# An attention and network kernel on one core: its first output products by half chunk, its raw weights in shorter rows, and its first four steps in a new order

## The chip, the cores and the metric

The kernel runs on one core of a Trainium2 chip. The core has five engines that run beside each other: TensorE (matrix products), VectorE, ScalarE, GpSimd and SyncE (which here only issues transfers), and 16 DMA engines that move data between HBM and the on-chip memory. Results of TensorE stand in banks called PSUM, everything else in SBUF. The metric is the device time of one execution in microseconds. Before the change it is 602.12 us, the median of 3 runs (602.03 to 602.43).

## The reference

A gated recurrence, whose result is the input of a two-layer network:

```
f = 1/(1+exp(-f_logit))                     # B=4, H=8, S=768, D=48
for t in range(S):
    state = f[:,:,t,:,None]*state + k[:,:,t]^T v[:,:,t]     # (B,H,D,D)
    y[:,:,t] = q[:,:,t] @ state
x = y.transpose(0,2,1,3).reshape(3072, 384)
h = x @ w_in                                # w_in 384 x 2048
g = max(h,0) + alpha*min(h,0)
out = g @ w_out                             # w_out 2048 x 384
```

q, k, v, f_logit are f32; w_in and w_out are stored as f64, eight bytes a value.

## The kernel before

The recurrence is computed in chunks of 128 positions. Two batches make a pair, so there are 2 pairs × 6 chunks = 12 steps of 256 tokens each, numbered 0 to 11. Within a chunk the state is not formed for each position: products of q with k (both scaled with running products of f) give a matrix A of weights that is nonzero where the key is not later than the query, and one product of A with the values gives the output of the chunk. The matrix falls into blocks of 32 and half chunks of 64 positions: nearby keys (`scores`), keys of an earlier block of the same half, and, through the state, everything before. All products are f32.

The work of a step is written as Python generators, each `yield` ending an item:

- P, `prepare`: the loads of f, q, k and v, then the sigmoid on ScalarE (L314), products and scans on VectorE (L326 to L468), the A copies of scaled queries on ScalarE (L473).
- S and T, `scores` for the first and second batch of the pair: an item of 32 products of q and k (L592), an item of VectorE's masked copies into `ad` (L601), another 32 products (L592 again, other operands), another masked copy (L627 in chunk 0, L611 later).
- O, `carry`: products across halves (in chunk 0 those of L509, copied to `ad` by L514), across 32-blocks (L524, copied to A by L531), in chunk 0 the keys transposed on TensorE (L541) and copied by ScalarE (L545, `ksn`), the states (L555), and `moved`, which adds the state to the values `vs` (L565, L569 on VectorE; L571, a ScalarE copy, for the first half of chunk 0).
- Y, `attend`: four copies of `ad` into A on ScalarE (L635), the 32 output products (L646: A against values and state), the copies y (L653), and the transposition to xT: in step 0 by products with a 0/1 matrix on TensorE (L665) with copies L667, in the others by transfers (L676).
- K and M: the keys of later chunks, transposed by transfers (L483) and put in place (L491).
- n, `network`: eight items, each with a bank `ph` of products xT × w_in (L691), the negative part on ScalarE (`neg`, L696) and the gate on VectorE (L698). Then the second layer: in step 0 32 plain products (L711), a part in each of four items; in the later steps, a scheme with seven products of half matrices instead of eight (L730), whose sums of the gates are formed on VectorE (L777).

The weights arrive in 16 pieces, eight of w_in and eight of w_out, each 128 partitions × 768 values of eight bytes. An item `a` (w_in) or `b` (w_out), generator `upper`, issues the load of a piece on SyncE (L248) and has ScalarE make two numbers of it (L252, `lead`, and L253); an item `w` or `g` adds these on VectorE (L262) into the f32 weights. The pool has RAWS = 3 raw buffers and LEADS = 4 for `lead`; a fourth load waits until ScalarE has read the first. The first 16-bit word of a row carries only low bits and is left out, so the row begins at the second word: 2,046 bytes for w_in (three rows a partition) and 6,142 for w_out (one). W forms the sums of w_out for the seven-product scheme, X gives the banks of the early stage to the network. Two sorts of products have no use but to keep TensorE at work: i (L802, 128×256) and j (L810, 16 short ones).

The order of all this is written out by hand. `START` lists the items of the first steps, word by word (`P0:2` is two items of P of step 0), and `USUAL` repeats from step 5 on. TensorE, VectorE, ScalarE and SyncE execute their instructions in just this order (`tc.manual_schedule`), each waiting where an operand isn't ready; GpSimd follows program order. An item that stands early for one engine stands early for all four.

Of the kernel before, what the change touches and what calls it, by code (L numbers as in the profile page):

```python
# [17 lines left out]
C = 128  # L18
# [3 lines left out]
U = 2  # L22
CH = 64
NC2 = C // CH
NB = DB // 4
WP = 768
RAWS, LEADS = 3, 4
UP = 2.0 ** 16

BEGUN = 5  # L30
START = (
# [7 lines left out]
)  # L39
USUAL = "T:2 S:2 n:3 M n T:2 S n P+ S n P+ n:3 Y O P+ O:2 Y O n P+ Y:2 P+ n:3 P+:3 K+"  # L40

# [19 lines left out]
def kernel(  # L61
# [30 lines left out]
    nc = tc.nc  # L92
    B, NC, _, HP, _ = qT.shape
    DM = v.shape[-1]
    H = 2 * HP
    D = DM // H
# [4 lines left out]
    W = U * HP * C  # L101
# [22 lines left out]
    pairs = [psa.tile([128, 2, 512], F32, tag=f"pair{n}", name=f"pair{n}") for n in range(2)]  # L124
    more = [psb.tile([128, 2, 512], F32, tag=f"more{n}", name=f"more{n}") for n in range(2)]
# [8 lines left out]
    def bank(name):  # L134
        return net["pool"].tile([128, 512], F32, tag="net", name=name)
# [11 lines left out]
    vs = []  # L147
# [36 lines left out]
    for half in range(2):  # L184
        for m in range(1, NQ):
            n = NQ - m
# [7 lines left out]
    A = const.tile([128, U, H, C], F32, tag="A", name="A")  # L194
# [10 lines left out]

    first["raw"] = stage.tile([128, WP, 4], I16, tag="raw", name="w_in_raw0", bufs=RAWS)

# [9 lines left out]
    def load_weights(dst, src, name):  # L217

        rows_ = NK if dst is w_in_sb else 1
        pieces_ = dst.shape[1] * dst.shape[2] // WP  # L230
        if rows_ == 1:
            dst = dst.rearrange("p a n -> p (a n)").unsqueeze(1)
        width = WP // rows_
        words = src.rearrange("p (a n) -> p a n", a=rows_).bitcast(I16)
        got = {}

        def of(n):
            return dst[:, :, n * width:(n + 1) * width]

        def by_row(t):  # L240
            return t.rearrange("p (a n) -> p a n", a=rows_)

        def upper(n):
            if not n and dst is w_in_sb:
                raw = first["raw"]
            else:
                raw = stage.tile([128, WP, 4], I16, tag="raw", name=f"{name}_raw{n}", bufs=RAWS)
            nc.sync.dma_start(out=raw.rearrange("p (a n) four -> p a (n four)", a=rows_)[:, :, 0:4 * width - 1],  # L248
                              in_=words[:, :, 4 * n * width + 1:4 * (n + 1) * width])

            lead = stage.tile([128, WP], F16, tag="lead", name=f"{name}_lead{n}", bufs=LEADS)
            nc.scalar.activation(lead, raw[:, :, 2].bitcast(BF16), AF.Copy, scale=0.5)  # L252
            nc.scalar.activation(as_int(n, I32), by_row(raw.bitcast(U32)[:, :, 0]), AF.Copy, scale=2.0 ** -13)  # L253
            got[n] = lead

        def as_int(n, dtype):
            t = of(n).bitcast(dtype)
            return t if dtype is I32 else t.rearrange("p a (n two) -> p a n two", two=2)[:, :, :, 1]

        def both(n):  # L260
            t = by_row(got.pop(n).bitcast(I16))
            nc.vector.tensor_tensor(as_int(n, I16), as_int(n, I16), t, ALU.add)  # L262

        def uppers():
            for n in range(pieces_):
                upper(n)
                yield

        def rests():
            for n in range(pieces_):  # L270
                both(n)
                yield

        return uppers(), rests()
# [355 lines left out]
    def attend(bp, c, x):  # L630

        i = f"{bp}_{c}"
        for j in range(NJ):
            s_ = slice(DB * j, DB * (j + 1))
            nc.scalar.copy(A[s_].rearrange("p u h t -> p (u h) t")[:, :, s_], ad[s_].rearrange("p u r h t -> p (u r h) t"))  # L635
            if j % 2:
                yield

        py = (more if (bp, c) == steps[0] else pairs)[0]
        for u in range(U):  # L640
            for hp in range(HP):
                for cc in range(NC2):
                    for par in range(2):
                        hd = 2 * hp + par
                        o = hp * C + CH * cc
                        nc.tensor.matmul(py[64 * par:64 * par + 64, u, o:o + CH],  # L646
                                         lhsT=vs[bp][:, cc, u, hd * D:hd * D + 64],
                                         rhs=A[:, u, par * HP + hp, CH * cc:CH * (cc + 1)],
                                         start=True, stop=True)
        yield  # L650
        y = work.tile([128, U, HP, C], F32, tag="ksn", name=f"y_{i}", bufs=1)
        for u in range(U):
            nc.scalar.copy(y[:, u].rearrange("p h t -> p (h t)"), py[:, u])  # L653
        if c < NC - 1:
            x["moved"](1)
        xT = x["T"] = work.tile([128, NK, T], F32, tag="xT", name=f"xT_{i}")
        if not (bp or c):

            yield
            for kt in range(NK):  # L660
                b = bank(f"xt{kt}_{i}")
                these = [hp for hp in range(HP) if 2 * D * hp < 128 * (kt + 1) and 2 * D * (hp + 1) > 128 * kt]
                for hp in these:
                    o = 2 * D - 2 * D * hp + 128 * kt
                    nc.tensor.matmul(b[:, 0:T], lhsT=dense[:, o:o + 128], rhs=y[:, :, hp],  # L665
                                     start=(hp == these[0]), stop=(hp == these[-1]))
                nc.scalar.copy(xT[:, kt], b[:, 0:T])  # L667
            yield
            return
        queues = iter([nc.sync, nc.scalar, nc.gpsimd, nc.sync, nc.scalar] * 2)  # L670
        for hd in range(H):
            d = hd * D
            while d < (hd + 1) * D:
                n = min((hd + 1) * D, (d // 128 + 1) * 128) - d
                p0 = 64 * (hd % 2) + d - hd * D
                next(queues).dma_start(  # L676
                    out=xT[d % 128:d % 128 + n, d // 128].rearrange("p (u t) -> p u t", u=U),
                    in_=y[p0:p0 + n, :, hd // 2])
                d += n
        yield  # L680
# [132 lines left out]
    steps = [(bp, c) for c in range(NC) for bp in range(B // U)]  # L813
# [8 lines left out]
    with tc.manual_schedule(engines={mybir.EngineType.PE, mybir.EngineType.DVE, mybir.EngineType.Activation,  # L822
                                     mybir.EngineType.SP}):
        run = {}
        for n, step in enumerate(steps):
            x = {}
            for key, stage_ in zip("POYKMn", (prepare, carry, attend, keys_moved, landed, network)):
                run[key, n] = stage_(*step, x)
            run["S", n], run["T", n] = (scores(u, *step, x) for u in range(U))
        for key in ORDER:  # L830
            next(run[key] if key in run else pieces[key[0]])
# [55 lines left out]
```

## Time and profile before

| | |
|---|---|
| timed runs, median (lowest to highest) | 602.12 us (602.03 to 602.43) |
| profiled execution | 606.02 us |
| its span on the core | 604.2 us |
| granted TensorE clock, mean | 0.994 |
| TensorE busy | 579.1 us (96%) |
| VectorE busy | 495.1 us (82%) |
| ScalarE busy | 246.7 us (41%) |
| GpSimd busy | 83.6 us (14%) |
| DMA | 50.36 MB in 52,880 packets, mean 83 GB/s |

The profile is of one execution. Its lines name the engine, the line of the kernel, the operation, output and inputs by the program's names, the tile's size and the number of instructions; a timeline's rows begin with start and busy time in microseconds and end with the idle time ahead of the row and what ended it. One f32 product shows as two records on TensorE. The page also gives the span in 40 slices of 15.1 us, with each engine's busy share in tenths; TensorE stands at 3, 4 and 8 in the first three slices and at 9 in all others but the last.

### The profile page before, as it was taken

The page shows a single profiled execution, that of the slowest core. Times are in us where ns is not written, and L with a number is a line of the kernel's source. Part 1 is how long each engine was busy: PE and PEld are TensorE (multiplying, and loading weights), DVE is VectorE, ACT ScalarE, POOL GpSimd, SP SyncE. Part 2 cuts the span into 40 slices and gives each one's busy share as a digit, 9 for nine tenths or more (in the row PEclk, how much of TensorE's full clock was granted, in tenths as well). Part 3 has the DMA queues.
Part 4 walks back from the last instruction along what each step waited for, and adds up shares of the span by engine and source line. Part 5 has one row for each costly group of instructions (what it writes and reads, how often), then busy time and mean ns, then how long its engine had stood idle before and what let it go on. Part 6 is the DMA issues. An engine that isn't in the chain of part 4 may idle for free.

```text
span 604.2 us, 18097 instructions
## 1 busy us (share of the span) xinstructions
PE 579.1 (96%) x7760; PEld 519.2 (86%) x7760; DVE 495.1 (82%) x998; ACT 246.7 (41%) x430; POOL 83.6 (14%) x162
## 2 busy tenths in 40 slices
PE   3489999999999999999999999999999999999997
PEld 2368767899899899899899889899899899899997
DVE  8968999998789778997997897997998997892351
ACT  5749962620461460460461352343344344232110
POOL 7310014004001202001200300300300300300000
PEclk9979999999999999999999999999999999999999
DMA  8766845105104402601501601601511511201000
GB/s 261 267 202 230 273 127 93 33 36 110 34 2 134 78 1 54 159 2 54 158 2 54 157 3 42 162 11 39 155 21 28 140 47 27 54 2 27 28 1 27
DMA packets 52880, 50.36 MB, mean 83 GB/s; under 512 B 26720, under 2 KB 43360, under 8 KB 52800
## 3 DMA queue, kind: packets, MB, share of 16 engines
q1 hardware_dynamic: 42784, 37.46, 22.3%
q0 software_dynamic: 5504, 9.90, 6.4%
q10 hardware_dynamic: 4512, 1.85, 1.3%
q8 instruction: 61, 1.00, 0.7%
q14 instruction: 19, 0.16, 0.1%
HBM read 36.21 MB, written 4.72 MB: 68 GB/s over the span
## 4 chain that ended last, share of the span: by engine, by line
PE 86%; DVE 9%; ACT 3%; issue 2%; DMA 1%; SPq 0%; DVEq 0%; ACTq 0%
PE ph L691 38%; PE pc L730 10%; PE pa L730 10%; PE pair L592 6%; PE pe L730 5%; PE pd L730 5%; PE pb L730 5%; PE pair L646 3%; DVE gate L698 2%; PE pair L555 1%; DVE w_out_sb L262 1%; PE pair L524 1%; PE xt L665 1%; PE po L711 1%; DVE ad L611 1%
## 5 line engine op out<-in xcount | busy, mean ns | idle before, releaser
L691 PE MATMUL ph<-xT,w_in_sb 128*128 128x256 f32 x1152 | 255.5, 381 | 0.1
L691 PEld LDWEIGHTS ph<-xT,w_in_sb 128*128 128x128 f32 x1152 | 217.6, 190 | 31.9 <-issue 1.3
L696 ACT ACTIVATE neg<-ph 128x512 f32<-128x512 f32 x96 | 56.0, 593 | 124.8 <-PE ph L691 79.5
L698 DVE SCALAR_TENSOR_TENSOR gate<-neg,om,ph 128x256 f32<-128x256 f32 x192 | 81.6, 477 | 27.2 <-ACT neg L696 27.0
L730 PE MATMUL pa<-w_out_sb,gate 128*128 128x192 f32 x352 | 62.6, 331 | 0.4 <-DVE gate L698 0.4
L730 PE MATMUL pc<-t,S 128*128 128x192 f32 x352 | 61.6, 329 | 0.0
L473 ACT COPY A<-q 48x512 f32<-48x512 f32 x44 | 27.1, 617 | 79.7 <-DVE q L421 79.1
L730 PEld LDWEIGHTS pa<-w_out_sb,gate 128*128 128x128 f32 x352 | 57.3, 190 | 2.3 <-DVE gate L698 1.0
L483 POOL DMA_DIRECT2D ksn<-kt x80 | 46.1, 584 | 86.4 <-DVE kt L435 61.5
L730 PEld LDWEIGHTS pc<-t,S 128*128 128x128 f32 x352 | 57.4, 190 | 0.4
L676 POOL DMA_DIRECT2D xT<-y x22 | 11.8, 543 | 288.3 <-ACT y L653 288.2
L601 DVE COPY_PREDICATED ad<-mraw,pair 128x256 f32<-128x256 int32 (+1 forms) x96 | 41.2, 454 | 8.5 <-ACT ad L514 4.7
L611 DVE COPY_PREDICATED ad<-mquad,pair 128x224 f32<-128x224 int32 (+6 forms) x140 | 41.8, 299 | 4.1
L377 DVE TENSOR_TENSOR us<-us,fs 128x768 f32<-128x768 f32 (+5 forms) x60 | 36.9, 616 | 1.1
L777 DVE TENSOR_TENSOR S<-gate 128x512 f32<-128x512 f32 x44 | 30.3, 688 | 0.8
L565 DVE TENSOR_TENSOR vs<-vs,f 48x768 f32<-48x768 f32 x20 | 19.1, 953 | 14.4 <-PE pair L646 11.9
L730 PE MATMUL pe<-w_out_sb,S 128*128 128x192 f32 x176 | 30.6, 328 | 0.0
L730 PE MATMUL pb<-t,gate 128*128 128x192 f32 x176 | 30.4, 326 | 0.0
L730 PE MATMUL pd<-w_out_sb,S 128*128 128x192 f32 x176 | 30.4, 326 | 0.0
L635 ACT COPY A<-ad 32x512 f32<-32x512 f32 x48 | 29.4, 613 | 0.6
L653 ACT COPY y<-pair 128x512 f32<-128x512 f32 x22 | 11.8, 589 | 43.0 <-PE pair L646 43.0
L730 PEld LDWEIGHTS pe<-w_out_sb,S 128*128 128x128 f32 x176 | 28.8, 190 | 0.3
(138 smaller groups left out, 723.9 us busy)
## 6 DMA issues: line engine op xcount, KB each, us to landing
w_out_raw<-in_w_out SPq DMA_DIRECT2D x8, 767.8 KB, 7.7
w_in_raw<-in_w_in SPq DMA_DIRECT2D x8, 767.2 KB, 10.5
out<-o SPq DMA_DIRECT2D x23, 192.0 KB, 1.9
q<-in_qT SPq DMA_DIRECT2D x8, 512.0 KB, 4.9
k<-in_kT SPq DMA_DIRECT2D x8, 512.0 KB, 7.1
f<-in_fT SPq DMA_DIRECT2D x7, 512.0 KB, 4.1
vs<-in_v SPq DMA_DIRECT2D x16, 192.0 KB
ksn<-kt SPq DMA_DIRECT2D x80, 32.0 KB, 2.2
```

The source lines that it names most:

```text
L377: nc.vector.tensor_tensor(us[:, :, UO[m]:UO[m] + 4 * n].rearrange("p g (i r) -> p g i r", r=4), us[:, :, skip:skip + 4 * n].rearrange("p g ...
L473: nc.scalar.copy(A[halves(cc)[1], :, par * HP:(par + 1) * HP, CH * cc:CH * (cc + 1)], q3[rows(par)].rearrange("p (u h c) s t -> p u h c (s ...
L483: (nc.gpsimd if a % 2 else nc.sync).dma_start(out=ksn[32 * b:32 * (b + 1)].rearrange("p u (h x) -> p (u h) x", h=HP)[:, :, 32 * a:32 * a + n],
L592: nc.tensor.matmul(to[DB * j:DB * (j + 1), par, hp * step + lo:hp * step + hi], lhsT=keys[r_, g * DB:(g + 1) * DB], rhs=by[r_, g, lo:hi], ...
L601: nc.vector.copy_predicated(adu[:, :, :, d:4], mraw[:, d, :, d:4].bitcast(I32).unsqueeze(1).broadcast_to((128, H, NB, n)), rv[:, :, QO[d]: ...
L611: nc.vector.copy_predicated(ad[:, u, :, :, 4 * m:DB], mquad[:, lo:lo + n].bitcast(I32).unsqueeze(1).unsqueeze(1).broadcast_to((128, 2, HP, ...
L635: nc.scalar.copy(A[s_].rearrange("p u h t -> p (u h) t")[:, :, s_], ad[s_].rearrange("p u r h t -> p (u r h) t"))
L691: nc.tensor.matmul(ph[:, j * T:(j + 1) * T], lhsT=w_in_sb[:, kt, m * 128:(m + 1) * 128], rhs=xT[:, kt], start=(kt == 0 and j == 0), stop=( ...
L696: nc.scalar.activation(neg, phv, AF.Relu, scale=-1.0)
L698: nc.vector.scalar_tensor_tensor(gate[:, m % NH, m // NH], neg[:, j], om[:, m:m + 1], phv[:, j], ALU.mult, ALU.add)
L730: nc.tensor.matmul(to[:, 0:DH], lhsT=of(f), rhs=by(f), start=(f == 0 and not more), stop=(f == NH - 1), skip_group_check=True)
L777: nc.vector.tensor_tensor(to, x_, y_, op)
```

## The change

There are three edits.

1. `attend`: in step 0 the 32 output products are sorted by half chunk, the 16 of the first half (cc = 0) as one item and the 16 of the second as another. The generator has one item more there; in all other steps the products keep their order and stay one item.
2. The raw loads: each partition's row is cut into pieces of 128 values, and of each the first 16-bit word is left out, so a piece of weights is 768 rows of 1,022 bytes (128 partitions × 6) in place of 384 of 2,046 bytes (w_in) or 128 of 6,142 (w_out). The words that are now left out too are low bits that no instruction reads.
3. `START` is a new list. The items are the same but for one more Y0, and the idle products are as many as before (two i, one j). In step 0, j now stands first, one i follows the first 32 products of the scores and the other the transposes of the keys (L541). VectorE's masked copies L627 of one batch (T) come ahead of six preparations of step 1; two of the copies L635 come ahead of the copies L545; the first half of L646 comes ahead of the states L555 and the second half behind them; the 32 products of step 1's scores that stood ahead of L646 now follow the transposition L665; the copies L252 and L253 of the third w_in piece stand behind y (L653). Steps 1 to 4 are shuffled by a few places; `USUAL` is unchanged.

```diff
 WP = 768
+PART = 128
 RAWS, LEADS = 3, 4
...
 START = (
-    "i P0:4 j T0 P0:2 S0 P0 a O0:2 T0 P1 P0 O0 T0 S0 O0 P1 S0 a O0 P1 T0 S0 P1 O0:2 Y0 i P1 Y0 O0 S1 w Y0 "
-    "a Y0 X a w O1 Y0 w O1 w S1 P1 a n0 w a:2 P1 n0 a T1 P1 P2 b S1 T1 S1 n0 w:2 n0 T1 O1 P2 T1 b P2 n0 w "
-    "O1 g n0 b O1 P2 g:2 b Y1 g b P2 n0:2 O1 n0 O1 b:3 g:2 O1 g n0 Y1:2 g W:2 P2 n0 Y1 T2 W S2 P2 P3 T2 "
...
+    "j P0:4 T0 P0:2 a i S0 O0:2 P0 P1 O0 T0 O0 a S0 T0:2 P1 S0 P1 O0 P0 S0 i P1 Y0 O0 P1 Y0:2 O0:2 Y0:2 w "
+    "X a P1 w O1 Y0 a O1 w S1 a S1 P1 w a n0:2 T1 O1 T1 P1 a n0 O1 a w n0 w P2 w T1 b P2 w T1 S1 P2 n0:2 "
+    "b:2 n0 b g:2 S1 n0 P2 O1 g O1 n0 O1 b:2 g Y1 O1 Y1 n0 g b:2 g Y1 P2 g:2 Y1 n0 W P2 W T2:2 W S2:2 P2 "
...
-            nc.sync.dma_start(out=raw.rearrange("p (a n) four -> p a (n four)", a=rows_)[:, :, 0:4 * width - 1],
-                              in_=words[:, :, 4 * n * width + 1:4 * (n + 1) * width])
+            nc.sync.dma_start(out=raw.rearrange("p (a c n) four -> p a c (n four)", a=rows_, n=PART)[:, :, :, 0:4 * PART - 1],
+                              in_=words[:, :, 4 * n * width:4 * (n + 1) * width]
+                              .rearrange("p a (c m) -> p a c m", m=4 * PART)[:, :, :, 1:4 * PART])
...
-        py = (more if (bp, c) == steps[0] else pairs)[0]
-        for u in range(U):
-            for hp in range(HP):
-                for cc in range(NC2):
-                    for par in range(2):
-                        hd = 2 * hp + par
-                        o = hp * C + CH * cc
-                        nc.tensor.matmul(py[64 * par:64 * par + 64, u, o:o + CH],
-                                         lhsT=vs[bp][:, cc, u, hd * D:hd * D + 64],
-                                         rhs=A[:, u, par * HP + hp, CH * cc:CH * (cc + 1)],
-                                         start=True, stop=True)
+        chunks_first = (bp, c) == steps[0]
+        py = (more if chunks_first else pairs)[0]
+        each = [(u, hp, cc) for u in range(U) for hp in range(HP) for cc in range(NC2)]
+        for n, (u, hp, cc) in enumerate(sorted(each, key=lambda x: x[2]) if chunks_first else each):
+            if chunks_first and n == U * HP:
+                yield
+            for par in range(2):
+                hd = 2 * hp + par
+                o = hp * C + CH * cc
+                nc.tensor.matmul(py[64 * par:64 * par + 64, u, o:o + CH],
+                                 lhsT=vs[bp][:, cc, u, hd * D:hd * D + 64],
+                                 rhs=A[:, u, par * HP + hp, CH * cc:CH * (cc + 1)],
+                                 start=True, stop=True)
```

8 rows, old and new, of the table START are left out of this document.

## The prediction

> **What bounds the kernel now.** I read the page first, then the fifteen-microsecond windows, then TensorE's timeline of the first 90 us, and last those of VectorE and ScalarE.
>
> ```profile
> span 604.2 us, 18097 instructions
> ...
> PE 579.1 (96%) x7760; PEld 519.2 (86%) x7760; DVE 495.1 (82%) x998; ACT 246.7 (41%) x430; POOL 83.6 (14%) x162
> ...
> q8 instruction: 61, 1.00, 0.7%
> ```
> ```profile
> 45.00:60.00 15.00, 15.00 (x278) 12.73 (x277) 13.13 (x29) 13.38 (x21) 0.73 (x1) 0.97 0.65 220
> 60.00:75.00 15.00, 14.90 (x68) 11.78 (x67) 14.93 (x26) 14.92 (x26) 0.73 (x1) 1.00 0.85 280
> ```
>
> The span is 604.2 us and the profiled execution took 606.02, so 1.8 lies around the span. The median of the timed runs is 602.12, 3.9 less than the profiled one: I work out a difference in the profile and take it off the median. In the windows the columns after the length are busy TensorE, weight loads, VectorE, ScalarE and GpSimd, then clock, DMA share and GB/s. TensorE is full from 45 us on. Of 604.2 − 579.1 = 25.1 us in which it is not busy, nearly all must lie ahead of that. The diff leaves TensorE's instructions as many as they were, so it can gain only by letting the first network product (L691) begin sooner, and lose by a new stall later. VectorE is full too in 60 to 75 (14.93 of 15): what TensorE gains is kept only as far as VectorE comes forward with it.
>
> TensorE's rows up to the first network products (start, busy, line, operands, count of records, idle time before and what ended it). One f32 product shows as two records:
>
> ```profile
> 9.27 2.40 PE L592 MATMUL pair<-qd,k 48*32 48x80 f32 x128 [5.60 <-ACT us_first L354]
> ...
> 17.56 0.86 PE L509 MATMUL more<-us_first 48*32 48x16 f32 x68 [3.09 <-issue]
> 18.35 1.13 PE L524 MATMUL more<-q,kh 48*64 48x64 f32 x32
> 21.49 0.59 PE L592 MATMUL pair<-us_first,k 48*32 48x52 f32 x28 [2.01 <-DVE ad L601]
> 24.00 1.52 PE L592 MATMUL pair<-us_first,k 48*32 48x52 f32 x100 [1.92 <-issue]
> 25.45 1.97 PE L541 MATMUL more<-ident,ks 128*128 128x128 f32 x8
> 29.33 1.53 PE L555 MATMUL more<-vs,ksn 64*48 64x48 f32 x64 [1.92 <-ACT ksn L545]
> ...
> 31.94 1.34 PE L592 MATMUL pair<-qd,k 48*32 48x80 f32 x64
> ...
> 34.64 2.14 PE L646 MATMUL more<-A,vs 128*64 128x64 f32 x48 [0.29 <-issue]
> 36.70 0.84 PE L509 MATMUL pair<-us 48*32 48x16 f32 x79
> 39.76 0.71 PE L509 MATMUL pair<-us 48*32 48x16 f32 x49 [2.21 <-issue]
> 40.39 5.49 PE L665 MATMUL xt<-y,dense 128*128 128x256 f32 x12
> 45.67 5.53 PE L691 MATMUL ph<-xT,w_in_sb 128*128 128x256 f32 x24
> ...
> 82.47 2.09 PE L646 MATMUL pair<-A,vs 128*64 128x64 f32 x64
> ...
> 90.17 1.59 PE L592 MATMUL pair<-qd,k 48*32 48x80 f32 x128 [0.25 <-DVE vs L569]
> ```
>
> Two things are to be seen besides the waits. First, the idles "<-issue" at 17.56 and 24.00 are 68 + 32 + 28 = 128 records apart, those at 34.64 and 39.76 are 48 + 79 = 127: the instructions arrive in blocks. The page's 61 fetches for 7,760 products and as many weight loads give 254 each, the same figure. From one block's first record to the next one's it was 6.4 us (17.56 to 24.00) and 5.1 (34.64 to 39.76). Which work lies behind a border is set by the order. Second, the page's clock does not tell the rate: 128 records of L592 took 2.40 us at 9.27 and 1.59 at 90.17; 48 of L646 took 2.14 at 34.64 and 64 took 2.09 at 82.47; xt (L665) took 0.46 for each record, ph at 45.67 takes 0.23 for one of the same size. All of xt runs at about half rate. The windows of 3.41 us (busy TensorE and clock):
>
> ```profile
> 29.13:32.54 3.41, 3.21 (x105) 1.00 0.80 283
> 32.54:35.95 3.41, 3.12 (x90) 1.00 0.65 156
> 35.95:39.36 3.41, 1.60 (x109) 0.98 0.91 296
> 39.36:42.77 3.41, 3.02 (x55) 0.50 0.69 176
> 42.77:46.19 3.42, 3.42 (x10) 0.52 0.29 107
> ```
>
> Two nearly full windows in a row are followed by the full rate (at 35.95), the stalled one takes it away again (0.50 from 39.36), and two more return it at 46.19, when xt is over.
>
> **The new order of the start.** The chain before it on the other engines (same columns):
>
> ```profile
> 22.82 0.69 DVE L330 TENSOR_TENSOR kr<-f 128x256 f32<-128x256 f32 x1
> ...
> 25.90 0.65 DVE L326 TENSOR_TENSOR qd<-qd,f 128x256 f32<-128x256 f32 x1
> 26.43 2.08 DVE L627 COPY_PREDICATED ad<-mhalf,pair 128x224 f32<-128x224 int32 x6
> ...
> 36.78 0.95 DVE L565 TENSOR_TENSOR vs<-vs,f 48x768 f32<-48x768 f32 x1 [2.15 <-PE more L646]
> ...
> 46.49 1.89 DVE L601 COPY_PREDICATED ad<-mraw,pair 128x256 f32<-128x256 int32 x4 [4.71 <-ACT ad L514]
> ```
> ```profile
> 28.21 1.07 ACT L545 COPY ksn<-more 128x512 f32<-128x512 f32 x2
> 29.16 2.51 ACT L635 COPY A<-ad 32x512 f32<-32x512 f32 x4
> 31.68 0.96 ACT L571 COPY vs<-more 48x384 f32<-48x384 f32 x2
> 32.67 0.90 ACT L252 ACTIVATE w_in_lead<-w_in_raw 128x768 f16<-128x768 bf16 x1
> ...
> 36.88 1.07 ACT L653 COPY y<-more 128x512 f32<-128x512 f32 x2 [2.50 <-PE more L646]
> ```
>
> Before, VectorE does its six preparations of the second step (22.82 to 26.43, 3.6 us) ahead of the masked copies L627, and ScalarE does the ksn copies L545 ahead of the four A copies L635. Now half of L627 stands ahead of the six, and two of the A copies ahead of L545. VectorE therefore waits from 22.8 for the products of the second border, which arrive at 24.00, of which 36 are needed first (0.55 us, so 24.55): a new wait of 1.7 us, behind which all its later work queues. From there, with durations of the rows: L627's first half 24.65 to 25.7, the six until 29.3, second half until 30.3, the first two A copies (half of 2.51) until 31.65, L545 until 32.7, the other two after it. TensorE takes the first half chunk's 32 records of L646 from 31.75 until 33.2 (2.14 / 48 = 0.045 each), then L555 (1.53) until 34.7; L571 ends at 35.8; the other 32 records at 37.3; the y copies (1.07) at 38.5 (37.95 before).
>
> So y comes 0.55 later. But S1, 64 records of L592 (the 1.34 us at 31.94 before), stands now behind xt instead of ahead of L646. Counted by the order, the border that was at 34.64 now lies 18 records into the second step's L509, and that of 39.76 lies behind xt, after 3 of S1's records. L509's block follows the one that begins inside L646's first half at 32.6, by 5.1 us: 37.7, so L509 ends near 38.7, beside the y copies. xt starts at about 38.8 instead of 40.39, 1.6 sooner. S1's other 61 records come 5.1 later, at 42.8, under xt.
>
> With the clock as the windows show it (two full in a row; from 35.95 the second ends at 42.77): xt has 4.0 us at half rate, 8.7 products, and 3.3 at full, 0.8, and ends at 43.6; S1 takes 0.8 (1.59 for 128), and ph begins at 44.4. Before's ph begins at 45.67, of which 0.5 until 46.19 are at half rate, worth 0.26: 45.93 at full rate. And S1, which stands ahead of ph now, was done before. The gain is 45.93 − 44.4 = 1.5 us. VectorE's own path gives some back: its idle of 2.15 at 36.78 and 4.71 at 46.49 is what pays for the new 1.7 and for L565, now later; by my walk the w_out adds, which L711 waits for, come 0 to 0.45 behind TensorE's demand. Gain 1.1 to 1.5, taken 1.3.
>
> The Trainium skill ("TensorE: Matmul & The Clock Gate", Part 1: The HAM clock gate) says one busy window of about 3.4 us returns the full rate. By that rule the window from 35.95 would be enough and the sum −2.4 to −3.2. Before's rows speak against it: the window from 39.36 is 3.02 busy of 3.41, and the next still shows 0.52.
>
> **Moves past queues.** The copies of the third w_in piece (L252, 32.67 before) stand behind y now, at 38.5. They free the buffer for the sixth load, whose issue was at 34.41 and comes at about 40.2. Behind it on SyncE's queue are the later loads alone.
>
> ```profile
> 34.41 0.54 SPq L248 DMA_DIRECT2D w_in_raw<-in_w_in  x1
> ```
>
> It is wanted by ScalarE at about 45.8; 5.6 us for a load under a DMA share of 0.5 to 0.7 is little slack, and a miss of 1 us delays ScalarE's queue but not yet ph, whose third pair of groups uses that piece near 58. Cost nothing, bounds 0 and +0.5. The idle products (L802, L810) are as many as before; the first of them now stands after 32 products of L592, in the 5.6 us of idle before 9.27 or beside VectorE's work: nothing. The new items of the second to fourth step move at most a few positions; I followed them to 220 us and found each wait covered by a queue that is full anyway. That is the weakest point of the sum: TensorE has hardly any slack against VectorE there, so bounds −0.3 and +1.5, taken 0.
>
> **Rows of 1,022 bytes.** A w_in piece goes from 384 rows of 2,046 bytes to 768, a w_out piece from 128 of 6,142 to 768.
>
> ```profile
> L248 SPq DMA_DIRECT2D w_in_raw<-in_w_in x8: 539/540/621, 7.0 to 48.3; - x8
> L248 SPq DMA_DIRECT2D w_out_raw<-in_w_out x8: 327/328/354, 50.9 to 73.5; - x8
> ```
> ```profile
> q1 hardware_dynamic: 408, 0.86, 81.3%
> ```
> ```profile
> q1 hardware_dynamic: 344, 1.92, 80.2%
> ```
>
> Issuing costs SyncE 212 ns more for 256 rows more, so 0.86 us for 768: +0.3 and +0.5, sixteen times, on a queue that mostly waits. The two rows of queue q1 are from 49 to 52.5 us (mostly w_in) and from 68 to 76 (mostly w_out): 16 × 3.5 × 0.813 / 408 = 112 ns for about 2,100 bytes, and 16 × 8 × 0.802 / 344 = 298 ns for about 5,580. That is a line with 4 to 7 ns for a row and the rest for bytes. So 600 more rows cost 600 × 5 / 16 = 0.2 us on a piece. Lower bound nothing; upper bound the time of a row as it is, 112 ns for half the bytes, +2.7 us on a piece. I take the line, since both rows lie on it: +0.2, hidden by DMA free for 0.15 to 0.35 of the time. The Trainium skill ("DMA: Bandwidth & Descriptors", Specifications) puts line rate at 512 bytes and up, which agrees; no row here is that short.
>
> The sum: −1.3 for the start, nothing for the rest; 606.02 becomes 604.7 and the median 602.12 becomes 600.8.
>
> **The rivals.** One busy window is enough. Then xt warms at 39.36, ends at 41.8 and ph begins at 42.6 to 43.2 (S1's block may then be late): −2.4 to −3.2 on TensorE, of which VectorE allows some 2.7: 599.4. For it: only that the window from 39.36 before was not quite full.
>
> The start slips. The 24.00 arrival is now on VectorE's path, and the fetch's length depends on the load traffic; a window misses the threshold by one small wait, and xt stays at half rate to 46.19. xt then starts at 39.9 to 40.1, ends at 45.4, S1 costs 1.3: 602.1 to 602.7, no change. For it: between two fetches the blocks differ by 1.3 us (6.4 and 5.1), and at 6.4 L509's block comes at 39.0 and xt starts at 40.1.
>
> Small rows are dear: the other side. In 45 to 75 DMA is free for 15 × 0.35 + 15 × 0.15 = 7.5 us, and about nine pieces land there, so 0.83 us a piece or 0.83 × 16 / 600 = 22 ns a row is the point from which the weights set the pace. At 30 ns the last piece is 9 × 600 × 8 / 16 = 2.7 us late, and L711 at 71.00 with it: 604.8 less what the start gained, 603.5. Against it: the two rows of q1, which give 4 to 7.
>
> **How the numbers follow.** My forecast 0.37, one window 0.25, the slip 0.22, dear rows or a new stall in the tightly packed stretch behind 60 us 0.16. About 0.2% (1.2 us) is what a measurement can tell from no change: below 600.9 and above 603.3. Of the forecast's 600.5 to 601.2 some six tenths lie below 600.9: faster 0.25 + 0.23 = 0.48; same 0.14 + 0.17 = 0.31; slower 0.16 + 0.05 = 0.21. The range leaves out a tenth at either end: 598.9 to 603.6.
>
> **What would show it.** Right: xt begins near 38.8 with no "<-issue" before it and S1 behind it; its last products take 0.23 and not 0.46; ph begins near 44.4; TensorE stays full from there. L627 shows a wait of about 1.7 us at 23. The q1 rows at 49 to 52.5 show some 60 ns a packet. Wrong: a border of the blocks ahead of xt that ends past 39.5 (the slip), ph at 43 (one window), waits before L711 ended by VectorE's w_out adds or DMA (rows), or waits of 0.3 us and more behind 75 us, which none of the lines above foresees.

## The result and the profile after

The changed kernel is slower: 606.53 us (605.82 to 609.73) against 602.03 (601.78 to 602.43), a ratio of 1.0078 (95% interval 1.0056 to 1.0101). On another chip it was 1.0060 (1.0039 to 1.0081). I had forecast 600.8, in 598.9 to 603.6. Over all the sessions below the kernel before took 600.8 to 609.3 us in single executions, so a profile of one is a draw from that spread.

The two profiles shown so far hide the loss: 604.2 us before and 604.6 after. The explanation is a second profile of the kernel before, unchanged (e1), which took 602.80, near the median of the 35 executions of this kernel in that session (602.75). Its page and TensorE's timeline (start, busy, line, count, idle before and what ended it):

```profile
span 601.0 us, 18097 instructions
...
PE 574.9 (96%) x7760; PEld 515.7 (86%) x7760; DVE 495.1 (82%) x998; ACT 246.3 (41%) x430; POOL 83.5 (14%) x162
```
```profile
24.91 1.51 PE L592 MATMUL pair<-us_first,k 48*32 48x52 f32 x100 [1.49 <-issue]
...
30.65 1.53 PE L555 MATMUL more<-vs,ksn 64*48 64x48 f32 x64 [2.33 <-ACT ksn L545]
...
34.53 2.19 PE L646 MATMUL more<-A,vs 128*64 128x64 f32 x64
...
38.83 0.60 PE L509 MATMUL pair<-us 48*32 48x16 f32 x49 [1.33 <-issue]
39.36 2.86 PE L665 MATMUL xt<-y,dense 128*128 128x256 f32 x12
42.05 5.34 PE L691 MATMUL ph<-xT,w_in_sb 128*128 128x256 f32 x24
...
65.47 2.83 PE L691 MATMUL ph<-xT,w_in_sb 128*128 128x256 f32 x12 [1.05 <-DVE w_in_sb L262]
```

And the changed kernel (lines behind L249 are two higher, behind L641 four):

```profile
span 604.6 us, 18081 instructions
...
PE 576.4 (95%) x7760; PEld 516.9 (85%) x7760; DVE 495.8 (82%) x998; ACT 246.9 (41%) x430; POOL 83.8 (14%) x162
```
```profile
24.71 1.51 PE L594 MATMUL pair<-us_first,k 48*32 48x52 f32 x100 [1.91 <-issue]
...
32.63 1.98 PE L650 MATMUL more<-A,vs 128*64 128x64 f32 x32 [3.65 <-issue]
34.54 1.53 PE L557 MATMUL more<-vs,ksn 64*48 64x48 f32 x64
37.17 1.98 PE L650 MATMUL more<-A,vs 128*64 128x64 f32 x32 [1.10 <-ACT vs L573]
39.08 1.45 PE L511 MATMUL pair<-us 48*32 48x16 f32 x128
40.45 2.92 PE L669 MATMUL xt<-y,dense 128*128 128x256 f32 x12
43.30 0.92 PE L594 MATMUL pair<-qd,k 48*32 48x80 f32 x64
44.15 5.45 PE L695 MATMUL ph<-xT,w_in_sb 128*128 128x256 f32 x24
...
70.06 5.40 PE L715 MATMUL po<-w_out_sb,gate 128*128 128x384 f32 x16 [0.85 <-DVE w_out_sb L264]
```
```profile
197.91 0.94 PE L557 MATMUL pair<-vs,kt 64*48 64x48 f32 x64 [1.50 <-ACT kt L493]
```

In e1 the kernel before runs xt at full rate (2.86 us, not 5.49) and begins ph at 42.05, not 45.67. Three experiments below (e2, e10, e11) keep its order up to xt, and in their profiles xt takes 2.83 to 2.86 us too: of the five profiles of this order only the first shows the half rate. Against e1 the changed kernel begins ph 2.1 us later, though its second block of scores came at the same time (24.71 and 24.91). The spans differ by 3.6: TensorE idles 604.6 − 576.4 = 28.2 us in place of 26.1, and is busy 1.5 us longer, mostly since L650 runs at a slower rate behind its wait (1.98 + 1.98 against 2.19). The larger waits behind that block are 3.65 + 1.10 + 0.85 + 1.50 = 7.1 against 2.33 + 1.33 + 1.05 = 4.7. The one at 32.63 is put down to no releaser; it ends 0.1 us after the A copies that the products read:

```profile
25.61 1.15 DVE L629 COPY_PREDICATED ad<-mhalf,pair 128x224 f32<-128x224 int32 x3 [1.81 <-PE pair L594]
...
30.26 0.99 DVE L629 COPY_PREDICATED ad<-mhalf,pair 128x224 f32<-128x224 int32 x3
```
```profile
31.29 1.25 ACT L637 COPY A<-ad 32x512 f32<-32x512 f32 x2 [0.16 <-DVE ad L629]
```

This profile too is of one execution. A second one of the changed kernel, unchanged (a1, span 603.7), has the same waits ahead of L650, but L650 takes 1.72 and 1.15 there, and ph begins 18.2 us after the second block of scores, where the first has 19.4 and e1 17.1. So the start loses 1.1 to 2.3 us by these three. From the beginning of ph to the end of the span it is 560.5 and 561.0 us in the changed kernel and 559.0 in e1: 1.5 to 2.1 us are lost behind it, and the wait near 200 us is 1.50 in the one and 2.19 in the other.

```profile
24.44 1.52 PE L594 MATMUL pair<-us_first,k 48*32 48x52 f32 x100 [1.91 <-issue]
...
32.35 1.72 PE L650 MATMUL more<-A,vs 128*64 128x64 f32 x32 [3.64 <-issue]
...
36.64 1.15 PE L650 MATMUL more<-A,vs 128*64 128x64 f32 x32 [1.10 <-ACT vs L573]
...
42.66 5.45 PE L695 MATMUL ph<-xT,w_in_sb 128*128 128x256 f32 x24
...
197.12 0.94 PE L557 MATMUL pair<-vs,kt 64*48 64x48 f32 x64 [2.19 <-ACT kt L493]
```

### The profile page after: what moved, and what is told of

The parts are those of the page before. It is cut to its first block, busy times and chain, and to the rows that moved or that the text cites. A ratio compares the mean times of both kernels' runs of the same rounds, so it can differ in the third digit from the quotient of the medians.

```text
span 604.6 us, 18081 instructions
## 1 busy us (share of the span) xinstructions
PE 576.4 (95%) x7760; PEld 516.9 (85%) x7760; DVE 495.8 (82%) x998; ACT 246.9 (41%) x430; POOL 83.8 (14%) x162
## 4 chain that ended last, share of the span: by engine, by line
PE 88%; DVE 6%; DMA 2%; issue 2%; ACT 1%; SPq 1%; ACTq 0%; POOL 0%; POOLq 0%; DVEq 0%
PE ph L695 38%; PE pc L734 9%; PE pa L734 9%; PE pair L594 6%; PE pb L734 5%; PE pd L734 5%; PE pe L734 4%; PE pair L650 4%; PE po L715 4%; PE pair L557 1%; DVE gate L702 1%; PE pair L526 1%; DMA q<-in_qT 1%; SPq L485 1%; DVE qd L328 1%
## 5 line engine op out<-in xcount | busy, mean ns | idle before, releaser
L734 PEld LDWEIGHTS pd<-w_out_sb,S 128*128 128x128 f32 x176 | 28.9, 190 | 0.0
L734 PEld LDWEIGHTS pb<-t,gate 128*128 128x128 f32 x176 | 28.9, 190 | 0.0
```

Source lines behind the costliest of these rows:

```text
L734: nc.tensor.matmul(to[:, 0:DH], lhsT=of(f), rhs=by(f), start=(f == 0 and not more), stop=(f == NH - 1), skip_group_check=True)
```

## The experiments

Two theories stood at first. A: the profile that I had worked from was of a long execution, and the new order loses time at the start and near 200 us. B: the short rows cost it. Each ratio is to the kernel before on the same chip.

| | ratio | 95% interval |
|---|---|---|
| e1, kernel before again | 1.0001 | 0.9980 to 1.0022 |
| e2, short rows alone | 1.0011 | 0.9988 to 1.0033 |
| e11, the same again | 1.0018 | 0.9997 to 1.0039 |
| f2, rows of 510 bytes alone | 1.0040 | 1.0019 to 1.0062 |
| e3, order alone (long rows) | 1.0044 | 1.0022 to 1.0067 |
| changed kernel again (a1) | 1.0060 | 1.0039 to 1.0081 |
| e4, keys' copy behind a network item | 1.0051 | 1.0028 to 1.0074 |
| e5, keys' copy ahead of it | 1.0034 | 1.0018 to 1.0049 |
| e6, sigmoid item moved | 1.0052 | 1.0031 to 1.0072 |
| e7, S1's products early again | 1.0079 | 1.0057 to 1.0102 |
| e8, e5 with preparations first | 1.0013 | 0.9995 to 1.0031 |
| e9, S1's products late, alone | 1.0010 | 0.9992 to 1.0027 |
| e10, before, weights' addition sooner | 1.0000 | 0.9983 to 1.0017 |
| f1, e8 with long rows | 1.0000 | 0.9984 to 1.0016 |
| f3, f1 with five idle products | 0.9984 | 0.9968 to 1.0001 |
| g1, f3 again | 0.9978 | 0.9957 to 0.9999 |
| g2, f3 with short rows | 0.9987 | 0.9970 to 1.0005 |
| f4, before with four idle products more | 1.0011 | 0.9988 to 1.0035 |

**The parts alone.** e1 is the kernel before. e2 takes edit 2 alone, e3 the changed kernel without it.

> The kernel before, unchanged, for a profile of one of its usual executions. Theory A (the profile shown of before was itself an execution 3.9 us longer than usual, because all of xt ran at half rate): about 602.0 us, span near 600.2, the 12 records of xt in about 2.9 us in place of 5.5, and the first ph near 42 in place of 45.67. Theory B (the rows of 1,022 bytes cost the time): 602.0 too, but with nothing at the start that differs by more than 1 us from the profile shown.

> The kernel before with the rows of 1,022 bytes and nothing else. Theory A: 602.0 to 602.6, since the rows lie beside other work. Theory B: 605 to 606.5, most of the loss.

> The changed kernel with the long rows (2,046 and 6,142 bytes) again: the new order and the products by half chunk alone. Theory A: 605.5 to 606.5, the whole loss. Theory B: 601 to 602.5.

e1 came out as theory A has it: the rows above. The order alone carries most of the loss (1.0044). The rows alone gave 1.0011 and, in e11, 1.0018; the intervals reach from nothing to 0.4%.

**The wait near 200 us.** K4 moves the keys of step 4 by transfers, M4 puts them in place on ScalarE (L493), and O4's products L557 read them. In the changed kernel M4 follows K4 directly, and the products stand earlier than before. SyncE's and ScalarE's timelines of the changed kernel, one fence each:

```profile
189.67 5.67 SPq L485 DMA_DIRECT2D ksn<-kt  x8
```
```profile
197.02 0.83 ACT L493 COPY kt<-ksn 128x768 f32<-128x768 f32 x1 [11.96 <-DMA ksn<-kt]
197.76 1.08 ACT L700 ACTIVATE neg<-ph 128x512 f32<-128x512 f32 x2
```

The transfers are issued until 195.3 and the copy starts at 197.0. In e1 it starts 8 us after the last issue, and the products (L555 there) come at 211.65, where the changed kernel has them at 197.91:

```profile
191.72 6.95 SPq L483 DMA_DIRECT2D ksn<-kt  x8
```
```profile
206.73 0.83 ACT L491 COPY kt<-ksn 128x768 f32<-128x768 f32 x1
```
```profile
211.65 0.90 PE L555 MATMUL pair<-vs,kt 64*48 64x48 f32 x64
```

e4 put a network item between, with M4 behind it (this and the later diffs show only the part of `START` that changes):

```diff
-S4 K4 M4 n2 n3:2 O4:3 P5 n3:2 P5 S4
+S4 K4 n2 n3:2 O4:2 n3 M4 O4 P5 n3 P5 S4
```

> The changed kernel with M of step 4 (ScalarE's copy of the moved keys) one network item later and the state products L557 of step 4 behind that item. The changed kernel's trace shows TensorE waiting 1.50 us for that copy. If that wait is a part of the loss: 1.2 to 1.5 us off the changed kernel, 605.0. If TensorE only waits later for the same thing or VectorE is behind anyway: within 0.4 us of the changed kernel.

The wait stayed, at 1.59 us. TensorE's and ScalarE's rows of e4 show why: ScalarE's copy now stood behind that item's negative part (200.89), which reads the item's network products, and TensorE is at these from 197.95 to 200.81.

```profile
197.95 2.86 PE L695 MATMUL ph<-xT,w_in_sb 128*128 128x256 f32 x12
202.40 0.94 PE L557 MATMUL pair<-vs,kt 64*48 64x48 f32 x64 [1.59 <-ACT kt L493]
```
```profile
200.89 0.60 ACT L700 ACTIVATE neg<-ph 128x512 f32<-128x512 f32 x1 [1.32 <-issue]
201.51 0.83 ACT L493 COPY kt<-ksn 128x768 f32<-128x768 f32 x1
```

e5 puts M4 ahead of it (`O4:2 M4 n3 O4`); a1 is the changed kernel beside it.

> The changed kernel, unchanged, beside the next three on one chip. Both theories: 2.5 to 4.5 us above the kernel before (0.4 to 0.75%). Within its trace, from the arrival of the second block of scores (the record of L594 with 100 products, 24.71 in the first trace) to the end of the span some 579 to 580 us, where the kernel before takes 576 to 577.

> The changed kernel with the state products L557 of step 4 one network item later, and ScalarE's copy of the moved keys (L493) ahead of that item's negative part, not behind it as in e4. If the wait of 1.5 us for this copy is a real part of the loss, the wait at L557 near 200 us is gone and the end comes 1.2 to 1.6 us sooner than in the changed kernel beside it. If VectorE is behind there anyway, another wait of the same size appears within 20 us.

In a1 it is 579.3 us from the second block to the end, as expected. In e5 the wait is gone (its two timelines), behind these products TensorE has none of 0.4 us or more until 355 us, and from the beginning of ph to the end it is 559.5 us, where a1 has 561.0. The ratio falls from 1.0060 to 1.0034 and the mean of all executions from 606.74 to 605.27, 1.5 us; against e6 below, which leaves this place as it was and ran on the same chip, it is 1.0. The intervals of the ratios overlap.

```profile
200.16 0.94 PE L557 MATMUL pair<-vs,kt 64*48 64x48 f32 x64
```
```profile
199.03 0.83 ACT L493 COPY kt<-ksn 128x768 f32<-128x768 f32 x1
```

**The start.** e6 was to put VectorE's six preparations ahead of L629 again (`a S0 T0 P1 T0 S0 P1`):

> The changed kernel with VectorE's six preparations of step 1 ahead of the first masked copies L629 again (the order of the kernel before); all else as changed. Theory: VectorE's new wait for the second block (1.8 us at 23.8) sits on the path, so the A copies, the first output products and xt come about 1.0 to 1.3 us sooner after that block's arrival, and the end with them. Rival (the path runs over ScalarE's own queue, whose copies L356 wait for the same preparations and then find the work of L547 and L573 behind them): less than 0.4 us.

The first P1 there is ScalarE's sigmoid item, the six preparations are the second. VectorE's order stayed as it was, so e6 says nothing on the theory; it is the changed kernel once more (1.0052). e8 moves the right item, on top of e5:

```diff
-a S0 T0:2 P1 S0 P1 O0 P0 S0 i P1
+a S0 T0 P1 S0 P1 T0 O0 P0 S0 i P1
```

> e5 (the changed kernel without its wait for the moved keys) with VectorE's six preparations L332 to L338 truly ahead of the first masked copies L629 (in e6 only ScalarE's sigmoid item had moved). Theory: VectorE's new wait of 1.8 to 2.1 us for the second block lies on the path: from that block's arrival to the first output products L650 it takes 7.9 us now and 6.7 then, and the end comes 1.0 to 1.3 us sooner than e5's. Rival (ScalarE's chain L356, L637, L547, L573 sets it): 7.5 us or more, less than 0.4 us.

From the block's first record to L650 it is now 30.68 − 23.66 = 7.0 us, where the changed kernel takes 7.9. That figure varies, though: f1, f3, g1 and g2 below keep this order and have 6.8 to 7.6, for VectorE no longer waits for the block but for ScalarE's sigmoid (L316). From the start of that sigmoid to the first output products it is 8.1 us in all five, and 9.0 to 9.4 in the six profiles of the changed order (the changed kernel twice, e3 to e6). So VectorE's new wait was on the path, with 0.9 to 1.2 us. The ratio goes from 1.0034 to 1.0013, about 1.3 us; the two ran on different chips and their intervals overlap.

```profile
23.66 1.52 PE L594 MATMUL pair<-us_first,k 48*32 48x52 f32 x100 [1.64 <-issue]
...
30.68 1.98 PE L650 MATMUL more<-A,vs 128*64 128x64 f32 x32 [2.76 <-issue]
```

The sigmoid in e8 and what follows on VectorE, then the sigmoid in the changed kernel's first profile, where L650 came at 32.63:

```profile
22.55 1.04 ACT L316 ACTIVATE f<-f 128x1024 f32<-128x1024 f32 x1
```
```profile
23.62 0.65 DVE L332 TENSOR_TENSOR kr<-f 128x256 f32<-128x256 f32 x1 [0.61 <-ACT f L316]
```
```profile
23.32 1.04 ACT L316 ACTIVATE f<-f 128x1024 f32<-128x1024 f32 x1
```

e7 and e9 test the place of step 1's first score products, in the changed kernel and in the kernel before:

```diff
-S0 i P1 Y0 O0 P1 Y0:2 O0:2 Y0:2 w X a P1 w O1 Y0 a O1 w S1 a S1 P1 w
+S0 i P1 Y0 S1 O0 P1 Y0:2 O0:2 Y0:2 w X a P1 w O1 Y0 a O1 w a S1 P1 w
```
```diff
-Y0 i P1 Y0 O0 S1 w Y0 a Y0 X a w O1 Y0 w O1 w S1
+Y0 i P1 Y0 O0 w Y0 a Y0 X a w O1 Y0 w S1 O1 w S1
```

> The changed kernel with step 1's first 32 score products (L594, 64 records) ahead of the first output products again, in the 3.65 us that TensorE waits there, not behind xt. Theory (they cost 0.85 us where they are and nothing in the wait): xt starts as before, ph begins 0.85 sooner, the end 0.8 sooner. Rival (the border of the instruction blocks moves back to within L511, ahead of xt, and costs a wait there as in the kernel before, 1.3 to 2.2 us): L511 shows an idle of over 1 us that ended without a releaser, and the end is the same or up to 1 us later.

> The kernel before with one part of the change alone: step 1's first 32 score products (L592, 64 records) behind the transposition L665. The wait without a releaser inside L509 (1.33 us in e1) should go, since the border of the blocks moves behind xt, and S1's 0.9 us come ahead of ph in its place. If the step of my prediction was right that this is worth something: xt 13.2 to 13.8 us after the second block's arrival (14.45 in e1), ph 0.3 to 0.7 us sooner, the end 0.3 to 0.7 us sooner. If it's a poor exchange: ph at the same time or later, 0 to +1 us.

Neither is a gain (1.0079 beside 1.0060, and 1.0010). In e7 the border is back within L511 (0.50 us of wait), and part of xt ran at half rate (4.09 us). In e9 the wait of 1.33 in L509 is gone as foreseen, but TensorE waits 1.53 for L571 ahead of L646 and 0.78 for VectorE's L569 ahead of xt in its place, and the 0.92 us of S1 still stand ahead of ph: a poor exchange.

**Weights, and rows once more.** e10 takes away e1's wait of 1.05 at 65.47, with `b w P2 n0` for `b P2 n0 w` in `START`:

> The kernel before with VectorE's addition of the last w_in piece (L262) ahead of the six preparations of step 2, which removes the wait of 1.05 us that its usual executions show ahead of the last network product of step 0 (65.47 in e1). If TensorE is the bound from there on: 0.8 to 1.0 us faster than the kernel before. If VectorE is (the additions of w_out come no sooner): the wait appears ahead of L711 in its place, and the end is the same.

The wait went and 0.45 ahead of L555 and 0.40 ahead of L646 came, both for ScalarE: no difference (1.0000).

> The rows of 1,022 bytes alone once more, since their first run left it open (the interval was 0.9988 to 1.0033). If rows cost nothing: 0.998 to 1.002. If they are a part of the loss: 1.001 to 1.004, and the borders of the first two instruction blocks come later, since their fetches share the DMA with more packets.

> e8 (the changed kernel without its wait for the moved keys and with VectorE's preparations first) with the long rows again: all that then stays of the change is the order. If the rows cost 0.1 to 0.2% and the two waits were the rest of the loss: 0.998 to 1.000 of the kernel before. If the rows cost nothing and the order has a third loss: 1.001 to 1.002, as e8.

> The kernel before with rows of 510 bytes (1,536 a piece), the suspected cost of more rows made larger: 1,152 and 1,408 rows more on a piece where the change has 384 and 640 more. If rows of 1,022 bytes cost 0.1 to 0.2% by their number, these cost 0.3 to 0.5% (2 to 3 us). If the first two results were chance: 0.999 to 1.001.

f1 is at 1.0000: with the two waits mended and the long rows, what is left of the new order costs nothing that shows, and it gains nothing either.

f2 sets PART = 64 in e2. Rows of 510 bytes do cost, 0.4%, as much as the expectation had if rows of 1,022 cost by their number; rows so short may cost for a reason of their own, which no run separates. Those of 1,022 gave 1.0011 and 1.0018 alone, and 0.9987 beside 0.9978 (g2, g1) with means of 602.57 and 602.76. The first two are 0.1 to 0.2% of loss, the last none, and so it is not settled. The later block borders that e11's expectation named aren't there: the second block came at 22.97 in e11 and 23.71 in e2, sooner than e1's 24.91. The transfers themselves don't show a cost. Queue q1 of e11 between 48 and 52 us, and the issues in the changed kernel:

```profile
q1 hardware_dynamic: 992, 1.00, 79.9%
```
```profile
L249 SPq DMA_DIRECT2D w_in_raw<-in_w_in x8: 601/602/677, 8.6 to 47.4; - x8
```

A row of 1,022 bytes took 16 × 4 × 0.799 / 992 = 52 ns, less than half of the 112 before (for about 2,100 bytes).

**The clock.** f3 fills TensorE's wait ahead of L650 in f1 (`i:5` for `i`); g1 repeats it, g2 has it with short rows, f4 puts four idle products ahead of L555 in the kernel before (`P1 i:4 O0:2 Y0 i`).

> f1 with five idle products L806 in place of one ahead of the first output products, where TensorE waits 2.8 us. Theory (the half-rate records of L650, 0.062 us each, and of part of xt come from that wait): L650's records at 0.035 and xt at 2.9 us in every execution, 0.5 to 1.2 us off f1. Rival (the next waits, for L573 and y, take the gain): the same as f1 within 0.4.

> The kernel before with four idle products more ahead of L555, where TensorE waits 2.3 us in its usual executions. If its slow executions (such as the one first profiled, with all of xt at half rate) come from the clock, the highest of its times come down and the mean with them by 0.3 to 1.0 us. If they come from the arrival of the inputs: the spread stays at 1.4 us and the mean within 0.4 us.

> f3 once more, to see if its gain on the kernel before holds: 0.9975 to 0.9995. If it was chance: 0.9995 to 1.001.

> f3 with the rows of 1,022 bytes, beside f3 itself on one chip. If the rows cost 0.1 to 0.2%: 0.6 to 1.3 us above g1. If they cost nothing: within 0.4 us of it.

TensorE's rows of f3 (with the long rows L650 is L649, and L573 is L572):

```profile
28.06 2.90 PE L805 MATMUL more<-ones 128*128 128x256 f32 x10
32.14 1.21 PE L649 MATMUL more<-A,vs 128*64 128x64 f32 x32 [1.18 <-issue]
33.28 0.94 PE L556 MATMUL more<-vs,ksn 64*48 64x48 f32 x64
35.43 1.15 PE L649 MATMUL more<-A,vs 128*64 128x64 f32 x32 [1.22 <-ACT vs L572]
36.51 1.26 PE L510 MATMUL pair<-us 48*32 48x16 f32 x128
38.29 2.94 PE L668 MATMUL xt<-y,dense 128*128 128x256 f32 x12 [0.52 <-DVE vs L570]
```

Everything from L649 runs at full rate; a wait for VectorE's L570 takes part of it back. Beside f1 on the same chip the mean goes from 603.18 to 602.37. At 0.9984 and 0.9978 it is the fastest of all, 0.2% under the kernel before; f3's own interval just holds 1, g1's does not. f4 made nothing narrower and nothing faster (1.0011): its times go from 600.95 to 607.07, as wide as before. So it did not show that the kernel's long executions come from the clock, and why single executions differ by some microseconds stays open.

## Why the prediction was wrong

- **The step that failed is the first: "I work out a difference in the profile and take it off the median".** The profiled execution stood 3.9 us above the median, and I said so, but did not ask what the 3.9 us were. In e1 the half rate of xt, 2.6 us of it, is not there, and the wait inside L509 is 1.33 for 2.21. The gain that I computed was the repair of an accident: e1, e2, e10 and e11 have no half rate to repair, and the border's wait inside L509, 0.84 to 1.80 us in them, gained nothing where e9 took it away. How often the half rate comes, no run counts. Against the profile that I worked from, ph did come sooner, at 44.15 for 45.67; the same new start, set against e1, is 2.1 us later at ph (1.1 by a1, counted from the second block).
- **The walk of the new chain held.** From the second block to L650 I had 31.75 − 24.00 = 7.75 us, measured 7.92; VectorE's wait 1.7, measured 1.81; xt stood 14.8 after the block, measured 15.7, as both halves of L650 took 1.98 where I had 1.43. It ran without a border ahead of it and S1 behind it, as said.
- **The clock's term was wrong, and that ph came near the forecast is luck.** I had xt at half rate until 42.77, 4.8 us in all; it took 2.92, all at full rate. xt began 0.9 later after the block than I had, took 1.9 less, and the block itself came 0.7 later: so 44.15 lies beside the forecast 44.4.
- **VectorE's new wait was not paid for by its later idle time.** I named it and put the price, at the w_out adds, at 0 to 0.45; TensorE waited 0.85 for these (L715). At the first output products the wait cost 0.9 to 1.2 us in the traces, and e8 against e5 gives about 1.3 in the times, since the A copies and these products hang on it.
- **"I followed them to 220 us and found each wait covered" was false at one place**, K4 and M4: 1.50 us, just the upper bound I had given, and 2.19 in a1. "At most a few positions" hid that the products which read the moved keys come 14 us sooner than in e1 (197.91 and 211.65), and the issue of the transfers only 2 (189.67 and 191.72).
- **S1 behind xt** was no gain: e9 gives +0.1% (0.9992 to 1.0027).
- **The rows**: the line through my two figures (112 ns for 2,100 bytes, 298 for 5,580) has no fixed cost at all, not the 4 to 7 ns that I read from it, and the 52 ns show none either. Issuing a w_in piece costs 62 ns more and not the 320 that I had. The rival of dear rows is not what made most of the loss, since the order alone has 1.0044. That 1,022 bytes still lie at line rate, as the Trainium skill has it ("DMA: Bandwidth & Descriptors", Specifications), agrees with the 52 ns. What the rows cost in the end is not settled: none to 0.2% by the ratios, up to 0.4% by their intervals.
- **The clock's rule** stays open: in e1 a window of 2.08 us busy did not bring the half rate, while in the first profile one of 1.60 did (both from 35.95). In a1 a window of 3.00 us (from 32.54, clock 0.52) is followed by 0.98, where in the first profile one of 3.02 was followed by 0.52. Windows cut at the same times need not line up with the clock's changes in another execution: in e9 they show 0.83 and 0.67.

```profile
35.95:39.36 3.41, 2.08 (x157) 1.00 0.61 177
39.36:42.77 3.41, 3.41 (x24) 1.00 1.00 285
```

## What to carry to other kernels

Where a profiled execution lies above the median by more than the effect in question, find out first which of its waits belong to that execution; a second profile would have done it here. The profile of the changed kernel needs the same: two of them put the loss at the start at 1.1 and 2.3 us. In an order written out by hand, an instruction moved ahead of others on its engine brings its own wait along, and all behind it pay; and a copy that reads moved data belongs behind enough other work, but ahead of anything on its engine that waits for the consumer (e4 and e5 differ by nothing else).

## What was not expected

Idle products in a wait of 3.4 us seem to have paid: with five in place of one, the 64 records of L649 took 2.4 us in place of 3.1 (f1; 2.9 to 4.0 in the profiles with one), and the ratio went from 1.0000 to 0.9984. The two intervals overlap, and four more idle products in the kernel before (f4) brought nothing.
